# Token-major block 0 of an S5 + GEGLU kernel: tile 3 taken last and from its DMA-turned form, its weight columns loaded in smaller pieces and on a second queue

## The chip, the cores and the metric
One core of a Trainium2 chip (trn2) runs the whole program. The metric is device time in microseconds (us); the figure for the kernel before is the median of three runs.

## The reference
One input x of 2048 tokens by 512 features is normalized (layernorm without gain), and three things are added: x itself, a diagonal complex state-space layer (S5), and a GEGLU feed-forward layer. Inputs and output are bfloat16.

```python
def _A_ref(x, ...):                       # S5, P = D = 512
    Lam_bar = jnp.exp(dt * Lam)
    B_bar = ((Lam_bar - 1.0) / Lam)[:, None] * Bmat
    Bu = jnp.einsum("bld,pd->blp", x + 0j, B_bar)
    h = Lam_bar[None, :] * h + Bu[:, t, :]          # for each t of 2048
    ...
    return 2.0 * jnp.einsum("blp,dp->bld", hseq, Cmat).real + x * Dskip

def _B_ref(x, w_gate, w_up, w_down):      # 512 -> 1376 -> 512
    return (_gelu(x @ w_gate) * (x @ w_up)) @ w_down

xn = _layernorm(x, axis=-1)
return x + _A_ref(xn, ...) + _B_ref(xn, ...)
```

## The kernel before
The 2048 tokens are four blocks of 512, each of four tiles of 128 tokens. For each block TensorE makes the gate and up products (`GU`), the input of the state-space layer (`BU`), and the down product with the state output (`DN`); VectorE runs the recurrence as scans (`CHAIN`), ScalarE applies gelu and empties PSUM.

In blocks 1 to 3, and for the hidden columns from 896 up in block 0, a matmul has the weights as its stationary operand and takes the *turned* normalized block `XNT[b]` (features on partitions). It is made by DMA: VectorE writes the normalized tile `XN` (`norms`, L634), and SyncE issues one DMA transpose per tile (`TR`, L736). That needs the statistics (`stats`, L615 and L616), the root on GpSimd (`root`, L621 to L623) and the reciprocal (`recip`, L627) first.

Block 0 is the start of the program, where the DMA engines bring the weights. Its hidden columns 0 to 895 are therefore made *token-major*: the tile of tokens is the stationary operand, and the weights stream past it, gate and up side by side in one PSUM bank. Four column groups `FR` of 256, 256, 256 and 128 are numbered u = 0 to 3. The tile is not yet normalized for this: VectorE only subtracts the mean (`cent` L962 for tiles 0 and 1, `sub` L951 for 2 and 3), TensorE turns it in four 128x128 pieces (`cent_T`, L684), ScalarE copies the turned tile to `XC` (L689), and the reciprocal of the standard deviation `rss[j]` goes in as the scale of gelu (L721) and of the multiply behind it (`GT_evac`, L724). `GT_k` (L701) is one matmul with one of the four slices of 128 features, so that it can start as soon as that slice of the weights has come; columns 0 to 511 of tiles 0 to 2 are made so. `GT_mm` (L712) is one accumulation of four matmuls. Ten of them follow: tile 3, columns 0 to 511, then columns 512 to 767 and 768 to 895 of tiles 0, 1, 2, 3. The hidden result goes to `H0` and is turned by DMA later (`H0_T`).

The gate and up weights come in parts: columns 0 to 511 slice by slice (`ld_wk`, L488, 128 KB each), then the ranges of `FC` (`ld_w`, L493): columns 512 to 895 (384 KB each) and 896 to 1375 (480 KB each, in `load_W`). All of these are issued by SyncE, and so run on DMA queue q1; the X tiles 1 and 2 and three parameter rows are issued by ScalarE, on q10. Behind the weights SyncE issues the transpose of the parameters (L515), the four DMA transposes of block 0's tiles, x of block 1 (L482) and the transposes of B (L526).

Order: the program lists operations, and a scheduler at build time gives each engine a fixed order. TensorE and SyncE keep the order of the listing; VectorE, ScalarE and GpSimd are ordered by modelled due times, save where `order_behind` (and `ch`, which chains VectorE's early operations) ties one behind another. Waits are semaphores; an engine that waits holds all that is behind it in its own order.

Of the kernel before, what the change touches and what calls it, by code (L numbers as in the profile page):

```python
# [9 lines left out]
ALU = mybir.AluOpType  # L10
ACTF = mybir.ActivationFunctionType
# [335 lines left out]
L, D, P, F = 2048, 512, 512, 1376  # L347
NT, NB, KD, KP, KF = 16, 4, 4, 4, 11
# [6 lines left out]
def d_pe(n_list):  # L355
    return sum(n / 2.4 + 2.5 for n in n_list)
def d_dve_tt2x(n): return 100.0 + 0.52 * n
def d_dve_1x(n): return 100.0 + 1.04 * n
# [3 lines left out]
def d_act(n, ptr=0): return 190.0 + 0.833 * n + 90.0 * ptr  # L362
# [3 lines left out]
def build(nc, ins, out):  # L366
    with ExitStack() as es:
        E = es.enter_context
        S = Sched(nc, es)
# [3 lines left out]
        PS = [E(nc.psum_tensor("PS%d" % i, [128, 512], F32)) for i in range(8)]  # L373
        BANK = [Buf("bank%d" % i, "ps", i, i + 1) for i in range(8)]
# [4 lines left out]
        WG = A.alloc("WG", [KD, F], BF16)  # L379
# [1 line left out]
        assert WG.lo == 0 and WU.lo == WG.hi  # L381
        WGU = arena_t[:, 0:2 * KD * F].rearrange("p (w k f) -> p w k f", w=2, k=KD)
        WD = A.alloc("WD", [KF, D], BF16)
        FC = [(0, 512), (512, 896), (896, F)]
        WGc = [Buf("WGc%d" % i, "sbx", 10 * i, 10 * i + 1) for i in range(KD + 2)]
        WUc = [Buf("WUc%d" % i, "sbx", 100 + 10 * i, 101 + 10 * i) for i in range(KD + 2)]
        wdeps = lambda Wc, ft: Wc[0:KD] if ft < 4 else [Wc[KD + (ft > 6)]]
        WDc = [Buf("WDc%d" % i, "sbx", 200 + 10 * i, 201 + 10 * i) for i in range(2)]
        XNT_all = A.alloc("XNT", [NB, KD, TB_], BF16)
        XNT = ring(XNT_all, "XNT", NB)  # L390
# [97 lines left out]
            return S.dma(lambda e: e.dma_start(W.ap[:, k, f0:f1], src[128 * k:128 * (k + 1), f0:f1]),  # L488
                         256 * (f1 - f0), writes=[Wc[k]], tag="ld_w")

        def ld_w(W, Wc, src, n):
            f0, f1 = FC[n]
            return S.dma(lambda e: e.dma_start(W.ap[:, :, f0:f1], src[:, f0:f1].rearrange("(k p) f -> p k f", p=128)),  # L493
                         1024 * (f1 - f0), writes=[Wc[KD + n - 1]], tag="ld_w")

        def ld_x0(j, queue="sync", after=()):
            return S.dma(lambda e, j=j: e.dma_start(X[j].ap, x2[128 * j:128 * (j + 1), :]), 128 * 1024, writes=[X[j]], tag="ld_x0", queue=queue, after=after)  # L497
# [2 lines left out]
        for k in range(KD):  # L500
# [1 line left out]
                ld_x0(k)  # L502
            ld_wk(WG, WGc, ins["B_w_gate"], k)
            ld_wk(WU, WUc, ins["B_w_up"], k)
        ld_w(WG, WGc, ins["B_w_gate"], 1)
        ld_w(WU, WUc, ins["B_w_up"], 1)

        def load_par():
            for q, nm in enumerate(("A_log_dt", "A_Lambda_re", "A_Lambda_im")):
# [17 lines left out]
                      1.4 * 512 * 1024, writes=[b_], tag="tr_" + nm, issue=3000.0)  # L527

        def load_W():
            ld_w(WG, WGc, ins["B_w_gate"], 2)  # L530
            ld_w(WU, WUc, ins["B_w_up"], 2)

        def load_B():
            load_T([A.sub(BBT_all, "BBTc%d" % c, c) for c in range(2)], ("A_B_re", "A_B_im"))
# [78 lines left out]
        def stats(b, j):  # L613
            tt = 4 * b + j
            return (S.order_behind(V(lambda e: e.bn_stats(ST[tt].ap, X[tt].ap), d_dve_1x(512), [X[tt]], [ST[tt]], "bnst"), GATE["hm"] if b else None),  # L615
                    V(lambda e: e.bn_aggr(MVt[b][j].ap, ST[tt].ap), D_TINY, [ST[tt]], [MVt[b][j]], "bnag"))  # L616
# [9 lines left out]
        def recip(qb, rq):  # L626
            return V(lambda e: e.reciprocal(rq.ap, qb.ap), 150, [qb], [rq], "rq")  # L627

        def norms(b, js, mn, rq, j0):
            last = None  # L630
            for j in js:
                tt, i = 4 * b + j, j - j0
                xs = XN[tt % 8]
                last = S.order_behind(V(lambda e, tt=tt, i=i, xs=xs: e.tensor_scalar(  # L634
                    xs.ap, X[tt].ap, mn.ap[:, i:i + 1], rq.ap[:, i:i + 1], ALU.subtract, ALU.mult),
                  d_dve_ts4x(512), [X[tt], mn, rq], [xs], "ln_n"), last)
            return last
# [66 lines left out]
        def GT_mm(j, u, bank):  # L704
            f0, f1 = FR[u]
            w = f1 - f0
            dst = PS[bank][:, 0:2 * w].rearrange("p (w f) -> p w f", w=2)

            def f(e):
                ins_ = None  # L710
                for k in range(KD):
                    ins_ = e.matmul(dst, XCd(j, k), WGU[:, :, k, f0:f1], start=(k == 0), stop=(k == KD - 1))  # L712
                return ins_
            PE(f, d_pe([2 * w] * KD), wdeps(WGc, 2 * u) + wdeps(WUc, 2 * u) + XCs[j], [BANK[bank]], "GT")

        def GT_evac(j, u, bank):
            f0, f1 = FR[u]
            w = f1 - f0
            GATE["nh"] = kk = (GATE["nh"] + 1) % 3
            sc, rb = rss[j]  # L720
            GATE["last_gelu"] = S.order_behind(ACT(lambda e: e.activation(GG[kk].ap[:, 0:w], PS[bank][:, 0:w], ACTF.Gelu_apprx_tanh, scale=sc),  # L721
                                                   d_act(w, 1), [BANK[bank], rb], [GG[kk]], "gelu"), GATE.get("last_gelu"))
            hp = Buf("H0_%d_%d" % (j, u), "sb", H0[j].lo + 2 * f0, H0[j].lo + 2 * f1)
            GATE["hm"] = S.order_behind(V(lambda e: e.scalar_tensor_tensor(H0[j].ap[:, f0:f1], PS[bank][:, w:2 * w], sc, GG[kk].ap[:, 0:w], ALU.mult, ALU.mult),  # L724
                                          d_dve_1x(w), [BANK[bank], GG[kk], rb], [hp], "hmul"), GATE.get("hm"))

        def H0_T():
            for j in range(4):
# [4 lines left out]
        def TR(b, js=range(4)):  # L733
            for j in js:
                tt = 4 * b + j
                S.dma(lambda e, b=b, j=j, tt=tt: e.dma_start_transpose(  # L736
                    XNT[b].ap[:, :, 128 * j:128 * (j + 1)], XN[tt % 8].ap),
                    1.6 * 128 * 1024, reads=[XN[tt % 8]], writes=[XTk[b][j]], tag="tr_x%d" % b, issue=1280.0)
# [67 lines left out]
        def GU_rest(b):  # L806
            k2, ft = b % 2, KF - 1
            f0, m = 128 * ft, FROWS[ft]
            for i in range(2):
                bank = next_bank()  # L810

                def f(e, i=i, bank=bank):
                    ins_ = None
                    for j in (2 * i, 2 * i + 1):
                        dst = PS[bank][:, 256 * (j % 2):256 * (j % 2) + 2 * m].rearrange("p (w f) -> p w f", w=2)
                        for dk in range(KD):
                            ins_ = e.matmul(dst, XNT[b].ap[:, dk, 128 * j:128 * (j + 1)], WGU[:, :, dk, f0:f0 + m],  # L817
                                            start=(dk == 0), stop=(dk == KD - 1))
                    return ins_
                PE(f, d_pe([2 * m] * 8), [WGc[KD + 1], WUc[KD + 1]] + XTr(b), [BANK[bank]], "GR%d" % b)  # L820
                GATE["nh"] = kk = (GATE["nh"] + 1) % 3
                g_, u_ = (PS[bank][:, :].rearrange("p (j x) -> p j x", j=2)[:, :, w * m:(w + 1) * m] for w in range(2))
                gs, us = (t[kk].ap[:, 0:2 * m].rearrange("p (j f) -> p j f", j=2) for t in (GG, UPB))
                GATE["last_gelu"] = ACT(lambda e, g_=g_, gs=gs: e.activation(gs, g_, ACTF.Gelu_apprx_tanh),
                                        d_act(2 * m), [BANK[bank]], [GG[kk]], "gelu", after=GATE["before_gelu"])
                ACT(lambda e, u_=u_, us=us: e.activation(us, u_, ACTF.Copy), d_act(2 * m), [BANK[bank]], [UPB[kk]], "evU")
                V(lambda e, i=i, gs=gs, us=us: e.tensor_tensor(HR.ap[:, 2 * i:2 * i + 2, 0:m], gs, us, ALU.mult),
                  d_dve_tt2x(2 * m), [GG[kk], UPB[kk]], [HRp[i]], "hmul")
            S.dma(lambda e: e.dma_start_transpose(HTt[k2][ft].ap.rearrange("p (j t) -> p j t", j=4), HR.ap),
                  1.2 * 128 * 1024, reads=HRp, writes=[HTt[k2][ft]], tag="tr_h%d" % b, issue=1200.0)  # L830
# [116 lines left out]
        def ch(*ops):  # L947
            for op in ops:
                tail_op[0] = S.order_behind(op, tail_op[0])
        def sub(j):  # L950
            return V(lambda e: e.tensor_scalar(XN[j].ap, X[j].ap, MVt[0][j].ap[:, 0:1], None, ALU.subtract),  # L951
                     d_dve_ts4x(512), [X[j], MVt[0][j]], [XN[j]], "sub")
# [39 lines left out]
        ch(*stats(0, 1))  # L992
        op, mn0, qb0, rq0 = root(0, 0, 3)
        ch(op)
        ch(*stats(0, 3)); ch(sub(3))
        ch(recip(qb0, rq0))
        op, mn3, qb3, rq3 = root(0, 3, 4)
        ch(op)
        rss = [(rq0.ap[:, i:i + 1], rq0) for i in range(3)] + [(rq3.ap, rq3)]
        for j in range(2):  # L1000
            ch(norms(0, [j], mn0, rq0, 0))
        ch(recip(qb3, rq3))
        TR(0, [0, 1])
        ks(1, 2, [0, 1])
        ks(2, 2, [0, 1])
        for j in range(3):
            GT_k(3, j, 0, [0, 1])
            if j == 0:
                cent_T(3, 0, 4, 6)
            GT_k(3, j, 1, [0, 1])  # L1010
            for u in range(2):
                GT_evac(j, u, acc(j, u))
        for (j, u), bank in zip([(3, 0), (3, 1), (0, 2), (0, 3), (1, 2), (1, 3), (2, 2), (2, 3), (3, 2), (3, 3)],
                                (6, 7, 0, 1, 2, 3, 4, 5, 0, 7)):
            GT_mm(j, u, bank)
            GT_evac(j, u, bank)
        rstate["n"] = 2
        norms(0, [2], mn0, rq0, 0)
        norms(0, [3], mn3, rq3, 3)
        TR(0, [2, 3])  # L1020
        ld_x(1)
        params()
        tables_dve(None)
# [87 lines left out]
```

## Time and profile before
| | us |
|---|---|
| median of three runs | 176.86 (176.77 to 177.54) |
| profiled execution, time | 177.26 |
| profiled execution, span | 175.9 |
| DMA traffic of block 0's stage, 4.4 to 13.2 | 281 and 322 GB/s in the two slices |
| last gate load (480 KB, issued 6.50), to landing | 6.8 |
| last up load (480 KB, issued 7.04), to landing | 7.6 |

Times inside the profile count from the start of the span. In the DMA view "to landing" counts from the start of the issue on the engine to the last of the data's arrival. SPq and ACTq are the sequencers of SyncE and ScalarE that issue DMAs; q1 and q10 are their DMA queues. Lines are those of the kernel before unless the text says otherwise; the change moves `GT_mm`'s matmul to L713 and `GU`'s to L851.

### The profile page before, as it was taken

How to read it: one execution, taken by the hardware profiler on the slowest of the kernel's cores; microseconds unless marked ns; L12 is line 12 of the kernel's file. 1: busy time of each engine (PE TensorE's matmuls, PEld its weight loads, DVE VectorE, ACT ScalarE, POOL GpSimd, SP SyncE). 2: the span in 40 equal slices, each digit the busy share in tenths (PEclk: the TensorE clock that was granted, in tenths of full speed). 3: DMA queues.
4: the chain of work that ended last, by engine and by line, in shares of the span. 5: the costliest groups of instructions: out<-in, count | busy, mean ns of one | idle time of the engine just before them, and what ended most of it. 6: DMA issues, size and time to landing. Idle time of an engine off the chain costs nothing.

```text
span 175.9 us, 2549 instructions
## 1 busy us (share of the span) xinstructions
PE 172.8 (98%) x903; PEld 85.4 (49%) x903; DVE 159.7 (91%) x279; ACT 95.8 (54%) x187; POOL 10.7 (6%) x24
## 2 busy tenths in 40 slices
PE   7999999999999999999999999999999999999995
PEld 2645664744544444444644444444464444444454
DVE  6797999987999989889899999989999899999941
ACT  5367668999766899383676793000667970000000
POOL 3132120211000000002200000000000000000000
DMA  5999989975899000002015000002004000000311
GB/s 144 281 322 154 216 136 203 174 132 114 162 270 270 11 0 2 0 30 75 18 33 112 5 0 4 0 0 89 30 0 34 0 0 0 0 0 4 119 62 60
DMA packets 32421, 14.36 MB, mean 82 GB/s; under 512 B 23737, under 2 KB 32409, under 8 KB 32409
## 3 DMA queue, kind: packets, MB, share of 16 engines
q1 hardware_dynamic: 31952, 13.84, 36.9%
q10 hardware_dynamic: 456, 0.36, 0.6%
q8 instruction: 7, 0.11, 0.3%
q14 instruction: 6, 0.04, 0.1%
HBM read 6.46 MB, written 2.10 MB: 49 GB/s over the span
## 4 chain that ended last, share of the span: by engine, by line
PE 95%; DMA 2%; SPq 1%; issue 0%; DVE 0%
PE PS L885 37%; PE PS L843 32%; PE PS L749 16%; PE PS L712 4%; PE PS L817 3%; PE PS L701 2%; DMA arena<-in_B_w_up_dram 2%; SPq L488 1%; PE PS L684 0%; SPq L497 0%; DVE arena L903 0%
## 5 line engine op out<-in xcount | busy, mean ns | idle before, releaser
L885 PE MATMUL PS<-arena 128*128 128x512 bf16 (+3 forms) x323 | 66.2, 366 | 0.0
L843 PE MATMUL PS<-arena 128*128 128x512 bf16 (+1 forms) x272 | 58.1, 373 | 0.0
L885 PEld LDWEIGHTS PS<-arena 128*128 128x128 bf16 (+1 forms) x323 | 30.8, 98 | 35.2
L843 PEld LDWEIGHTS PS<-arena 128*128 128x128 bf16 x272 | 26.5, 98 | 29.5
L787 DVE TENSOR_TENSOR_SCAN arena<-arena 128x512 bf16<-128x512 f32 x32 | 38.9, 1256 | 0.0
L859 ACT ACTIVATE arena<-PS 128x512 bf16<-128x512 f32 x33 | 19.8, 599 | 26.2 <-DVE arena L903 16.7
L749 PE MATMUL PS<-arena 128*128 128x512 bf16 (+1 forms) x144 | 28.3, 355 | 0.1
L863 ACT ACTIVATE arena<-PS 128x512 bf16<-128x512 f32 x33 | 19.8, 599 | 5.4 <-PE PS L843 5.4
L749 PEld LDWEIGHTS PS<-arena 128*128 128x128 bf16 x144 | 14.0, 98 | 13.7 <-DMA arena<-arena 0.6
L877 ACT ACTIVATE PS<-arena 128x512 f32<-128x512 bf16 (+2 forms) x17 | 9.6, 582 | 19.7 <-DVE arena L903 19.0
L758 ACT ACTIVATE arena<-PS 128x512 bf16<-128x512 f32 x32 | 17.6, 597 | 1.6 <-PE PS L749 1.6
L903 DVE TENSOR_TENSOR arena<-PS,arena 128x512 bf16<-128x512 f32 (+2 forms) x17 | 10.9, 654 | 6.4 <-PE PS L885 6.4
L865 DVE TENSOR_TENSOR arena<-arena 128x512 bf16<-128x512 bf16 x33 | 13.2, 419 | 2.1 <-ACT arena L863 2.0
L776 DVE TENSOR_TENSOR arena<-arena 128x4096 bf16<-128x4096 bf16 (+1 forms) x5 | 9.2, 1859 | 0.4 <-ACT arena L611 0.4
L799 DVE TENSOR_TENSOR arena<-arena 128x4096 bf16<-128x4096 bf16 x4 | 9.2, 2291 | 0.1
L774 DVE TENSOR_TENSOR arena<-arena 128x4096 bf16<-128x4096 bf16 (+1 forms) x5 | 9.2, 1861 | 0.0
L800 DVE TENSOR_TENSOR arena<-arena 128x4096 bf16<-128x4096 bf16 x4 | 9.1, 2287 | 0.0
L615 DVE BATCH_NORM_STATS2 arena<-arena 128x6 f32<-128x512 bf16 x12 | 7.8, 685 | 0.9 <-DMA arena<-in_A_x_dram 0.7
L721 ACT ACTIVATE arena<-PS,arena 128x256 bf16<-128x256 f32 (+1 forms) x16 | 6.5, 450 | 3.3 <-DVE arena L621 1.5
L712 PE MATMUL PS<-arena 128*128 128x512 bf16 (+1 forms) x40 | 7.1, 336 | 0.0
L701 PE MATMUL PS<-arena 128*128 128x256 bf16 (+1 forms) x36 | 6.2, 308 | 0.2 <-DMA arena<-in_B_w_up_dram 0.2
L724 DVE SCALAR_TENSOR_TENSOR arena<-PS,arena 128x256 bf16<-128x256 f32 (+1 forms) x16 | 6.2, 444 | 0.0
(95 smaller groups left out, 124.2 us busy)
## 6 DMA issues: line engine op xcount, KB each, us to landing
out_dram<-arena SPq DMA_DIRECT2D x15, 128.0 KB, 1.7
arena<-in_A_x_dram SPq DMA_DIRECT2D x3, 512.0 KB, 6.3
arena<-in_B_w_down_dram SPq DMA_DIRECT2D x1, 1280.0 KB, 8.8
arena<-in_B_w_gate_dram SPq DMA_DIRECT2D x4, 128.0 KB, 3.4
arena<-in_B_w_up_dram SPq DMA_DIRECT2D x4, 128.0 KB, 3.6
arena<-in_B_w_gate_dram SPq DMA_DIRECT2D x1, 480.0 KB, 6.8
arena<-in_B_w_up_dram SPq DMA_DIRECT2D x1, 480.0 KB, 7.6
arena<-arena SPq DMA_TRANSPOSE x25, 3.3
```

The source lines that it names most:

```text
L701: PE(lambda e: e.matmul(dst, XCd(j, k), WGU[:, ws[0]:ws[-1] + 1, k, f0:f1], start=first, stop=k == KD - 1, skip_group_check=True), d_pe([w ...
L712: ins_ = e.matmul(dst, XCd(j, k), WGU[:, :, k, f0:f1], start=(k == 0), stop=(k == KD - 1))
L749: ins_ = e.matmul(PS[bank][:, 128 * j0:128 * j1], BBT[c][dk].ap[:, 128 * s:128 * (s + 1)], XNT[b].ap[:, dk, 128 * j0:128 * j1], start=(dk ...
L758: GATE["evBu"] = ACT(lambda e, bank=bank, k3=k3, s=s, c=c: e.activation(SSc[k3][s][c].ap, PS[bank][:, :], ACTF.Copy), d_act(512), [BANK[ba ...
L787: V(lambda e, g=g, rb=rb, init=init: e.tensor_tensor_scan(g.ap, rb, g.ap, init, ALU.mult, ALU.add), d_dve_scan(512), [g, PA[RRr]] + ([CARc ...
L843: ins_ = e.matmul(PS[bank][0:m, c0:c1], W.ap[:, dk, 128 * ft:128 * ft + m], XNT[b].ap[:, dk, c0:c1], start=(dk == 0), stop=(dk == KD - 1))
L859: GATE["last_gelu"] = ACT(lambda e, bg=bg, kk=kk, m=m: e.activation(GG[kk].ap[0:m, :], PS[bg][0:m, :], ACTF.Gelu_apprx_tanh), d_act(512), ...
L863: ACT(lambda e, bu=bu, kk=kk, m=m: e.activation(UPB[kk].ap[0:m, :], PS[bu][0:m, :], ACTF.Copy), d_act(512), [BANK[bu]], [UPB[kk]], "evU")
L865: V(lambda e, kk=kk, m=m, ft=ft, k2=k2: e.tensor_tensor(HTt[k2][ft].ap[0:m, :], GG[kk].ap[0:m, :], UPB[kk].ap[0:m, :], ALU.mult), d_dve_tt ...
L877: ACT(lambda e: e.activation(PS[bank][:, c0:c1], X[tt].ap[:, c0:c1], ACTF.Copy), d_act(c1 - c0), [X[tt]], [BANK[bank]], "seed")
L885: ins_ = e.matmul(PS[bank][:, c0:c1], l_[:, 128 * j:128 * (j + 1)], r_[:, c0:c1], start=False, stop=last and n == len(ops) - 1, skip_group ...
L903: V(lambda e: e.tensor_tensor(OUTB[ko].ap[:, c0:c1], PS[bank][:, c0:c1], XD[tt].ap[:, c0:c1], ALU.add), d_dve_1x(c1 - c0), [BANK[bank], XD ...
```

## The change
Six edits, all in block 0. (1) The columns 512 to 895 are loaded as 512 to 767 and 768 to 895, two loads for each of gate and up. (2) The up load of columns 896 to 1375 goes from SyncE's queue to ScalarE's, behind the eviction of turned tile 2. (3) Tile 3 is no longer centred by VectorE, turned by TensorE and copied by ScalarE. (4) `GT_mm` of tile 3 takes the DMA-turned, normalized tile, so that its gelu and multiply have no scale. (5) The order of the ten `GT_mm` is: columns 512 to 767 of tiles 0, 1, 2, then 768 to 895 of tiles 0, 1, 2, then tile 3 with all four groups; the banks follow, and the bank counter behind them starts at 0. (6) The tiles' DMA transposes are issued in the order 0, 3, 1, 2. In the fixed order of VectorE, tile 2 is normalized ahead of tile 3, and all four ahead of the first multiply.

```diff
--- before.py
+++ after.py
@@ -381,10 +381,10 @@
         assert WG.lo == 0 and WU.lo == WG.hi
         WGU = arena_t[:, 0:2 * KD * F].rearrange("p (w k f) -> p w k f", w=2, k=KD)
         WD = A.alloc("WD", [KF, D], BF16)
-        FC = [(0, 512), (512, 896), (896, F)]
-        WGc = [Buf("WGc%d" % i, "sbx", 10 * i, 10 * i + 1) for i in range(KD + 2)]
-        WUc = [Buf("WUc%d" % i, "sbx", 100 + 10 * i, 101 + 10 * i) for i in range(KD + 2)]
-        wdeps = lambda Wc, ft: Wc[0:KD] if ft < 4 else [Wc[KD + (ft > 6)]]
+        FC = [(0, 512), (512, 768), (768, 896), (896, F)]
+        WGc = [Buf("WGc%d" % i, "sbx", 10 * i, 10 * i + 1) for i in range(KD + 3)]
+        WUc = [Buf("WUc%d" % i, "sbx", 100 + 10 * i, 101 + 10 * i) for i in range(KD + 3)]
+        wdeps = lambda Wc, ft: Wc[0:KD] if ft < 4 else [Wc[KD + (ft > 5) + (ft > 6)]]
         WDc = [Buf("WDc%d" % i, "sbx", 200 + 10 * i, 201 + 10 * i) for i in range(2)]
         XNT_all = A.alloc("XNT", [NB, KD, TB_], BF16)
         XNT = ring(XNT_all, "XNT", NB)
@@ -488,10 +488,10 @@
             return S.dma(lambda e: e.dma_start(W.ap[:, k, f0:f1], src[128 * k:128 * (k + 1), f0:f1]),
                          256 * (f1 - f0), writes=[Wc[k]], tag="ld_w")
 
-        def ld_w(W, Wc, src, n):
+        def ld_w(W, Wc, src, n, queue="sync"):
             f0, f1 = FC[n]
             return S.dma(lambda e: e.dma_start(W.ap[:, :, f0:f1], src[:, f0:f1].rearrange("(k p) f -> p k f", p=128)),
-                         1024 * (f1 - f0), writes=[Wc[KD + n - 1]], tag="ld_w")
+                         1024 * (f1 - f0), writes=[Wc[KD + n - 1]], tag="ld_w", queue=queue)
 
         def ld_x0(j, queue="sync", after=()):
             return S.dma(lambda e, j=j: e.dma_start(X[j].ap, x2[128 * j:128 * (j + 1), :]), 128 * 1024, writes=[X[j]], tag="ld_x0", queue=queue, after=after)
@@ -502,8 +502,9 @@
                 ld_x0(k)
             ld_wk(WG, WGc, ins["B_w_gate"], k)
             ld_wk(WU, WUc, ins["B_w_up"], k)
-        ld_w(WG, WGc, ins["B_w_gate"], 1)
-        ld_w(WU, WUc, ins["B_w_up"], 1)
+        for n in (1, 2):
+            ld_w(WG, WGc, ins["B_w_gate"], n)
+            ld_w(WU, WUc, ins["B_w_up"], n)
 
         def load_par():
             for q, nm in enumerate(("A_log_dt", "A_Lambda_re", "A_Lambda_im")):
@@ -527,8 +528,7 @@
                       1.4 * 512 * 1024, writes=[b_], tag="tr_" + nm, issue=3000.0)
 
         def load_W():
-            ld_w(WG, WGc, ins["B_w_gate"], 2)
-            ld_w(WU, WUc, ins["B_w_up"], 2)
+            ld_w(WG, WGc, ins["B_w_gate"], 3)
 
         def load_B():
             load_T([A.sub(BBT_all, "BBTc%d" % c, c) for c in range(2)], ("A_B_re", "A_B_im"))
@@ -709,20 +709,28 @@
             def f(e):
                 ins_ = None
                 for k in range(KD):
-                    ins_ = e.matmul(dst, XCd(j, k), WGU[:, :, k, f0:f1], start=(k == 0), stop=(k == KD - 1))
+                    xs = XCd(j, k) if j < 3 else XNT[0].ap[:, k, 128 * j:128 * (j + 1)]
+                    ins_ = e.matmul(dst, xs, WGU[:, :, k, f0:f1], start=(k == 0), stop=(k == KD - 1))
                 return ins_
-            PE(f, d_pe([2 * w] * KD), wdeps(WGc, 2 * u) + wdeps(WUc, 2 * u) + XCs[j], [BANK[bank]], "GT")
+            PE(f, d_pe([2 * w] * KD), wdeps(WGc, 2 * u) + wdeps(WUc, 2 * u) + (XCs[j] if j < 3 else [XT0[j]]), [BANK[bank]], "GT")
 
         def GT_evac(j, u, bank):
             f0, f1 = FR[u]
             w = f1 - f0
             GATE["nh"] = kk = (GATE["nh"] + 1) % 3
-            sc, rb = rss[j]
-            GATE["last_gelu"] = S.order_behind(ACT(lambda e: e.activation(GG[kk].ap[:, 0:w], PS[bank][:, 0:w], ACTF.Gelu_apprx_tanh, scale=sc),
-                                                   d_act(w, 1), [BANK[bank], rb], [GG[kk]], "gelu"), GATE.get("last_gelu"))
             hp = Buf("H0_%d_%d" % (j, u), "sb", H0[j].lo + 2 * f0, H0[j].lo + 2 * f1)
-            GATE["hm"] = S.order_behind(V(lambda e: e.scalar_tensor_tensor(H0[j].ap[:, f0:f1], PS[bank][:, w:2 * w], sc, GG[kk].ap[:, 0:w], ALU.mult, ALU.mult),
-                                          d_dve_1x(w), [BANK[bank], GG[kk], rb], [hp], "hmul"), GATE.get("hm"))
+            gate, up, g, h = PS[bank][:, 0:w], PS[bank][:, w:2 * w], GG[kk].ap[:, 0:w], H0[j].ap[:, f0:f1]
+            if j < 3:
+                sc, rb = rss[j]
+                fg = lambda e: e.activation(g, gate, ACTF.Gelu_apprx_tanh, scale=sc)
+                fh = lambda e: e.scalar_tensor_tensor(h, up, sc, g, ALU.mult, ALU.mult)
+                rb = [rb]
+            else:
+                fg = lambda e: e.activation(g, gate, ACTF.Gelu_apprx_tanh)
+                fh = lambda e: e.tensor_tensor(h, up, g, ALU.mult)
+                rb = []
+            GATE["last_gelu"] = S.order_behind(ACT(fg, d_act(w, 1), [BANK[bank]] + rb, [GG[kk]], "gelu"), GATE.get("last_gelu"))
+            GATE["hm"] = S.order_behind(V(fh, d_dve_1x(w), [BANK[bank], GG[kk]] + rb, [hp], "hmul"), GATE.get("hm"))
 
         def H0_T():
             for j in range(4):
@@ -817,7 +825,7 @@
                             ins_ = e.matmul(dst, XNT[b].ap[:, dk, 128 * j:128 * (j + 1)], WGU[:, :, dk, f0:f0 + m],
                                             start=(dk == 0), stop=(dk == KD - 1))
                     return ins_
-                PE(f, d_pe([2 * m] * 8), [WGc[KD + 1], WUc[KD + 1]] + XTr(b), [BANK[bank]], "GR%d" % b)
+                PE(f, d_pe([2 * m] * 8), [WGc[KD + 2], WUc[KD + 2]] + XTr(b), [BANK[bank]], "GR%d" % b)
                 GATE["nh"] = kk = (GATE["nh"] + 1) % 3
                 g_, u_ = (PS[bank][:, :].rearrange("p (j x) -> p j x", j=2)[:, :, w * m:(w + 1) * m] for w in range(2))
                 gs, us = (t[kk].ap[:, 0:2 * m].rearrange("p (j f) -> p j f", j=2) for t in (GG, UPB))
@@ -992,32 +1000,31 @@
         ch(*stats(0, 1))
         op, mn0, qb0, rq0 = root(0, 0, 3)
         ch(op)
-        ch(*stats(0, 3)); ch(sub(3))
-        ch(recip(qb0, rq0))
+        S.order_behind(ld_w(WU, WUc, ins["B_w_up"], 3, "scalar"), GATE["evTA"])
+        ch(*stats(0, 3))
         op, mn3, qb3, rq3 = root(0, 3, 4)
         ch(op)
-        rss = [(rq0.ap[:, i:i + 1], rq0) for i in range(3)] + [(rq3.ap, rq3)]
-        for j in range(2):
-            ch(norms(0, [j], mn0, rq0, 0))
+        ch(recip(qb0, rq0))
+        rss = [(rq0.ap[:, i:i + 1], rq0) for i in range(3)]
+        ch(norms(0, [0], mn0, rq0, 0))
+        ch(norms(0, [1], mn0, rq0, 0))
         ch(recip(qb3, rq3))
-        TR(0, [0, 1])
+        ch(norms(0, [3], mn3, rq3, 3))
+        TR(0, [0, 3, 1])
         ks(1, 2, [0, 1])
         ks(2, 2, [0, 1])
         for j in range(3):
             GT_k(3, j, 0, [0, 1])
-            if j == 0:
-                cent_T(3, 0, 4, 6)
             GT_k(3, j, 1, [0, 1])
             for u in range(2):
                 GT_evac(j, u, acc(j, u))
-        for (j, u), bank in zip([(3, 0), (3, 1), (0, 2), (0, 3), (1, 2), (1, 3), (2, 2), (2, 3), (3, 2), (3, 3)],
-                                (6, 7, 0, 1, 2, 3, 4, 5, 0, 7)):
+        for (j, u), bank in zip([(0, 2), (1, 2), (2, 2), (0, 3), (1, 3), (2, 3), (3, 0), (3, 1), (3, 2), (3, 3)],
+                                (6, 7, 0, 1, 2, 3, 4, 5, 6, 7)):
             GT_mm(j, u, bank)
             GT_evac(j, u, bank)
-        rstate["n"] = 2
+        rstate["n"] = 0
         norms(0, [2], mn0, rq0, 0)
-        norms(0, [3], mn3, rq3, 3)
-        TR(0, [2, 3])
+        TR(0, [2])
         ld_x(1)
         params()
         tables_dve(None)
```

## The prediction
> **What bounds the kernel now.** I read the page's busy shares first, then the chain of work that ended last in order of time, then SyncE's timeline and the DMA view in narrow windows. On the page:
>
> ```profile
> PE 172.8 (98%) x903; PEld 85.4 (49%) x903; DVE 159.7 (91%) x279; ACT 95.8 (54%) x187; POOL 10.7 (6%) x24
> ```
>
> TensorE is busy for 172.8 of 175.9 us, so an edit pays only by taking work or a wait from TensorE, and a new TensorE wait is paid almost in full. The chain over the changed stage and its first pause afterwards (start us, length us, what):
>
> ```profile
> 7.86 1.89 PE PS L701 x9
> 9.75 0.34 PE PS L684 x4
> 10.09 1.08 PE PS L701 x5
> 11.16 6.93 PE PS L712 x40
> 18.09 5.20 PE PS L843 x32
> ...
> 31.52 0.12 issue
> ```
>
> L684 x4 is tile 3 being turned on TensorE. L712 x40 are ten whole accumulations (`GT_mm`): 24 matmuls of 512 columns and 16 of 256. Block 0's token-major work ends at 18.09, and what follows runs back to back but for 0.12 us at 31.52. The question is therefore when L843 can start in the changed kernel.
>
> SyncE's timeline (start, length, what) and the DMA view of single issues (size, us from issue to landing) give the data's side:
>
> ```profile
> 4.98 0.45 SPq L488 DMA_DIRECT2D arena<-in_B_w_up_dram  x1
> 5.47 0.43 SPq L493 DMA_DIRECT2D arena<-in_B_w_gate_dram  x1
> 5.95 0.51 SPq L493 DMA_DIRECT2D arena<-in_B_w_up_dram  x1
> 7.82 1.99 SPq L515 DMA_TRANSPOSE arena<-arena  x1
> 10.27 5.15 SPq L736 DMA_TRANSPOSE arena<-arena  x4
> ```
>
> ```profile
> arena<-in_B_w_up_dram SPq DMA_DIRECT2D x1, 128.0 KB, 3.8
> arena<-in_B_w_up_dram SPq DMA_DIRECT2D x1, 384.0 KB, 6.0
> arena<-arena SPq DMA_TRANSPOSE x1, 5.0
> arena<-arena SPq DMA_TRANSPOSE x1, 4.1
> ```
>
> Issue plus landing time: the last 128 KB up chunk arrives at 8.8, the 384 KB up chunk at 11.95. The first two turned tiles, issued at 10.27 and about 11.6, arrive at 15.3 and 15.7: they wait behind 960 KB of weights on the same queue, so their arrival is set by the DMA engines, not by their issue.
>
> **The change, part by part.** *Removed from TensorE:* four turns of tile 3, 0.34 us of the chain. The twelve L701 matmuls around them then follow each other, and the first `GT_mm` could start at 9.75 + 1.08 = 10.83. Forty matmuls remain after it, 6.93 us. With no wait L843 starts at 17.76, a gain of 0.33.
>
> *First new wait, the weights of columns 512 to 767.* Before, the first two `GT_mm` (tile 3, columns 0 to 511) needed only weights long there, and columns 512 and up were first touched at 11.16 + 8 matmuls of 0.217 = 12.9, 0.95 after their arrival at 11.95. Now tile 0 columns 512 to 767 comes first, at 10.83. Its two loads are 256 KB instead of 384 KB, with the same 1024 row pieces. The two old loads took 11.95 - 8.8 = 3.15 us; the new take 2.1 by bytes and 3.15 by pieces. I take 2.4, nearer to bytes, as the share of busy DMA engines follows the bytes moved elsewhere in this stretch. That alone gives 11.2.
>
> Then comes the third up chunk, 480 KB, on ScalarE's queue. It stands behind the last eviction of tile 2 (second L689 of the pair at 7.73) and waits for nothing, so it is issued near 8.0 and moves data from about 9.0, by the 0.9 us between X tile 0's issue at 0.74 and the first DMA traffic. What a second queue does to SyncE's queue can be seen where X tile 2 came on ScalarE's queue. The DMA view of 4.4 to 5.2 (packets, MB, share of 16 engines), and below it that of 5.4 to 6.2:
>
> ```profile
> q1 hardware_dynamic: 163, 0.15, 55.6%
> q10 hardware_dynamic: 126, 0.11, 46.2%
> ```
>
> ```profile
> q1 hardware_dynamic: 265, 0.24, 98.8%
> q10 hardware_dynamic: 5, 0.00, 1.5%
> ```
>
> Beside q10, q1 moves 0.15 MB where alone it moves 0.24, a factor of 0.62. At 9.0 the new chunk still needs 2.2 us alone, 2.2 / 0.62 = 3.5 beside q10; q10's 0.49 MB at 0.11 per 0.8 us last 3.6, so the whole of it is shared. Arrival: 12.5. The ends: by bytes 1.9 / 0.62 gives 12.1, by pieces 13.3; unshared, 10.9. I take 12.4. TensorE then waits 1.6 us at its first `GT_mm`, and the forty matmuls end at 12.4 + 6.93 = 19.3.
>
> The Trainium skill, "DMA: Bandwidth & Descriptors", Queues, rings and completion order, says that each DMA engine takes turns between queue rows packet by packet. By that rule the 960-byte pieces of ScalarE's load would take more than the equal share seen above from 512-byte pieces, and the arrival would be about 12.8, 0.4 later than my sum; no stretch of this trace has unequal pieces on the two queues, so the trace leaves it open; the sum would be 178.4, inside the forecast's own range.
>
> *Second new wait, the turned tile 3.* Its four accumulations come last and need the DMA-turned tile. Up to there TensorE has 3 x 0.87 + 3 x 0.43 = 3.9 us of `GT_mm`, so it asks for it at 14.7 without the first wait and at 16.3 with it. VectorE normalizes tiles 0, 1, 2 and then 3 before the hmuls: reciprocal at 9.55, three L634 to about 10.8, L627 at 10.85, L634 done near 11.4. So the tile is issued second, at about 11.6, where the old second one stood. It arrived at 15.7; q1 ahead of it and q10 together hold the same bytes, but the old pair of 384 KB loads has become four, two of them 128 KB in rows of 256 bytes. The window 14 to 15, nearly all 256-byte pieces of turns, moved at up to 282 GB/s, so these 256 KB take 0.93. With the 2.4 above that is 3.33 against 3.15 for the old pair: 15.9. The ends: by bytes 15.7, and with the first pair by pieces (3.15) 16.6. I take 15.9. This is under the 16.3, so it adds nothing to the sum, but it would bind at 14.7 if the first wait went away.
>
> *Hidden:* SyncE issues two loads more and one fewer at a pitch of 0.48; the PAR transpose moves to about 8.3 and ends at 10.3, where tile 0's turn stood anyway (10.27). ScalarE issues its load in 0.65 us of an idle stretch of 1.46 (before 9.85), and loses one eviction of 0.59. VectorE loses one subtract (0.35); its hmuls start near 11.4 at 0.39 each, and the first bank they must free (0) is asked for after 2 x 0.87 us of `GT_mm`, 12.6 at the earliest, when it is free. The exp of the parameters waits for the PAR transpose (15.0 before, up to 0.8 later), and L558 on VectorE behind it; queued behind L558 are the hmuls of tiles 1 to 3, and their banks 2 to 7 are asked for by L843 after 20. Without that cover each 0.1 of delay costs 0.1. The gelu without scale and the plain multiply are off the path: 0.
>
> *Sum:* 19.3 - 18.09 = +1.2, less the pause of 0.12 at 31.52, which a later TensorE uses up: +1.1 us. The profiled execution took 177.26 with its span of 175.9, so it would be 178.4; from the median of 176.86, which lies 0.4 lower, it is 178.0.
>
> **Rivals.**
> *Not slower: both transfers land in time.* If the chunk is there by 10.83 and the tile by 14.7, the turns' 0.33 and the 0.12 are won: 176.4. For it: a smaller first chunk, and 480 KB taken off the queue ahead of the turned tile. Against it: the unshared bound is already 10.9, and the tile would have to come a full us before the 15.7 of its predecessor in the same place. It decides at 11.16 for the chunk and 15.1 for the tile: later than either, the wait has eaten the 0.33.
> *The tile alone binds.* If the second queue fills idle DMA time (261 GB/s on the mean from 6.2 to 10.0, against 335 from 4.4 to 5.2 with both queues), the chunk lands by 11.5 and the tile at 15.7 to 16. L843 then starts 3.02 us (the last 12 x 0.217 + 4 x 0.105) after the tile: 18.7 to 19.0, +0.5 to +0.8 with the pause: 177.5.
> *The short rows bind.* The two loads of columns 768 to 895 lie ahead of the tile in q1. The window 14 to 15 moved 172 GB/s on the mean, and only 282 in its busy part. At 172 their 256 KB take 1.52: the tile comes at 16.5 to 17.2, say 16.9, and L843 at 19.9: +1.8, less the pause: 178.5.
> The Trainium skill, "DMA: Bandwidth & Descriptors", Specifications, wants pieces of 512 bytes or more for the full rate, a rule that speaks against this load; the 282 GB/s of the trace beside its 305 with long rows (5.4 to 6.2) speaks against much of a loss, and the rival has a chance of 0.1.
>
> **How the numbers follow.** Forecast 0.57 (two waits, 177.5 to 178.7); tile alone 0.2; in time 0.13; short rows 0.1. A measurement here tells 0.5% (0.9 us) from no change, so slower begins at 177.7. Of the forecast 0.8 lies above, 0.46; of the tile alone a quarter, 0.05; the short rows whole, 0.1: slower 0.61. In time is a gain of 0.3% and counts as the same: with the rest of the others, 0.36. Faster by 0.9 us would take more than the turns and all pauses of the stage: 0.03. The range leaves out the lower part of in time and little of the first wait's far end: 176.6 to 179.0. The forecast's own is 177.5 to 178.7.
>
> **What would show it.** L713 (the old L712) starts near 12.4 after a wait for the up load, and L851 (the old L843) near 19.3. ScalarE's load is issued near 8.0. The turned tile 3 lands near 16. No L684 x4 after 9. From L851 on everything is as before, shifted by 1.1. Wrong is: a first `GT_mm` before 11.2, a PE wait of under 0.3 in 10 to 19, or L851 before 18.

## The result, and the profile after

The changed kernel takes 177.75 us (median of 22 runs, 177.03 to 178.67) against 177.09 of the kernel before in the same runs (176.59 to 177.57): a ratio of 1.0037, 95% interval 1.0024 to 1.0051. It is slower by 0.66 us, less than the 0.5% that the prediction took as the bound of what can be told; 22 runs of each tell it. Ratios and intervals leave out slow runs, those more than 1.5% above the fastest of their kernel; only e4 below has any, three of its twelve.

The page of the profiled execution (178.04 us, span 176.7), and TensorE's timeline (start, length, line, count, idle time before and its releaser):

```profile
PE 172.2 (97%) x884; PEld 86.0 (49%) x899; DVE 159.7 (90%) x278; ACT 95.0 (54%) x186; POOL 9.6 (5%) x24
```

```profile
7.62 0.39 PE L684 MATMUL PS<-arena 128*128 128x128 bf16 x4
7.85 3.13 PE L701 MATMUL PS<-arena 128*128 128x256 bf16 x14
10.81 4.06 PE L713 MATMUL PS<-arena 128*128 128x512 bf16 x24
15.93 3.20 PE L713 MATMUL PS<-arena 128*128 128x512 bf16 x16 [1.05 <-DMA arena<-arena]
18.96 5.36 PE L851 MATMUL PS<-arena 128*128 128x256 bf16 x31
```

TensorE has four matmuls less to do (899, of which 884 left a record) and is idle longer. The turn of tile 3 is gone, and the first `GT_mm` starts at 10.81. Then TensorE stands for 1.05 us ahead of tile 3's sixteen matmuls. The chain of what ended last shows the wait from the DMA's side, and where block 0's token-major work ends (19.13, against 18.09 before; the chain counts a matmul from the end of the one before it, the timeline from its own start, so that the same L851 stands there at 18.96):

```profile
11.73 4.15 DMA arena<-arena
15.88 0.05 issue
15.93 3.20 PE PS L713 x16
19.13 1.75 PE PS L851 x16
```

The next L851 of the chain begins at 39.50, against 38.74 before, a delay of 0.76: of the 1.04, 0.28 is taken up between. The pause of 0.12 that the kernel before had at 31.52 is part of that; the rest was not traced. The ends of the two spans differ by 0.8.

The data's side, by the DMA view of single issues: the two pieces of columns 512 to 767 (issued at 5.48 and 5.96), and the up load on ScalarE's queue (8.05):

```profile
arena<-in_B_w_gate_dram SPq DMA_DIRECT2D x1, 256.0 KB, 3.8
arena<-in_B_w_up_dram SPq DMA_DIRECT2D x1, 256.0 KB, 4.2
...
arena<-in_B_w_up_dram ACTq DMA_DIRECT2D x1, 480.0 KB, 6.6
```

The chunk arrives at 10.2, 0.6 ahead of its first use. The second queue came too late to hurt it: it has no traffic in the DMA view of 8.4 to 10.0 (the first line below), and half of it from 10.5 to 13.0:

```profile
q1 hardware_dynamic: 1208, 0.45, 108.4%
```

```profile
q10 hardware_dynamic: 459, 0.43, 54.1%
q1 hardware_dynamic: 504, 0.42, 49.3%
```

### The profile page after: what moved, and what is told of

It is laid out like the page before. It is cut to its first block, busy times and chain, and to the rows that moved or that the text cites. A ratio compares the mean times of both kernels' runs of the same rounds, so it can differ in the third digit from the quotient of the medians.

```text
span 176.7 us, 2528 instructions
## 1 busy us (share of the span) xinstructions
PE 172.2 (97%) x884; PEld 86.0 (49%) x899; DVE 159.7 (90%) x278; ACT 95.0 (54%) x186; POOL 9.6 (5%) x24
## 4 chain that ended last, share of the span: by engine, by line
PE 87%; DMA 2%; ACT 2%; issue 1%; DVE 0%; DVEq 0%
PE PS L893 37%; PE PS L851 32%; PE PS L757 13%; PE PS L825 3%; DMA arena<-arena 2%; PE PS L713 2%; ACT arena L766 1%; ACT arena L610 1%; DVE arena L726 0%; DVE arena L911 0%; DVEq L341 0%
## 5 line engine op out<-in xcount | busy, mean ns | idle before, releaser
L851 PE MATMUL PS<-arena 128*128 128x512 bf16 (+1 forms) x265 | 57.3, 373 | 0.4
L851 PEld LDWEIGHTS PS<-arena 128*128 128x128 bf16 x272 | 26.6, 98 | 29.5
L757 PE MATMUL PS<-arena 128*128 128x512 bf16 (+1 forms) x142 | 28.1, 355 | 0.1
L757 PEld LDWEIGHTS PS<-arena 128*128 128x128 bf16 x144 | 14.1, 98 | 13.3
L713 PE MATMUL PS<-arena 128*128 128x512 bf16 (+1 forms) x40 | 7.3, 337 | 1.1 <-DMA arena<-arena 1.1
L713 PEld LDWEIGHTS PS<-arena 128*128 128x128 bf16 x40 | 3.8, 98 | 4.5 <-DMA arena<-arena 1.3
L825 PE MATMUL PS<-arena 128*128 128x192 bf16 x64 | 5.9, 246 | 0.0
```

What stands on the lines that cost most here:

```text
L713: ins_ = e.matmul(dst, xs, WGU[:, :, k, f0:f1], start=(k == 0), stop=(k == KD - 1))
L757: ins_ = e.matmul(PS[bank][:, 128 * j0:128 * j1], BBT[c][dk].ap[:, 128 * s:128 * (s + 1)], XNT[b].ap[:, dk, 128 * j0:128 * j1], start=(dk ...
L851: ins_ = e.matmul(PS[bank][0:m, c0:c1], W.ap[:, dk, 128 * ft:128 * ft + m], XNT[b].ap[:, dk, c0:c1], start=(dk == 0), stop=(dk == KD - 1))
```

## The experiments

In all kernels below but the loads-only pair, every engine's order is that of the changed kernel except for the loads that are named; they were moved after the orders had been fixed. Ratios are to the kernel before on the same chip, whose median was 177.17 (e1 to e4), 177.10 (e5 to e8) and 177.04 us (e9 to e12); they were not taken from the two medians, whose quotient is at times another (1.0062 for e5, where the ratio is 1.0080).

**Without the tile wait (e1).**
```diff
-                    xs = XCd(j, k) if j < 3 else XNT[0].ap[:, k, 128 * j:128 * (j + 1)]
+                    xs = XCd(min(j, 2), k)
...
+            if o.tag == "GT":
+                o.deps = [d for d in o.deps if d.tag != "tr_x0"]
```


> The changed kernel, with tile 3's four accumulations reading tile 2's centred, TensorE-turned copy instead of their own DMA-turned tile (so tile 3's hidden columns 0 to 895 are not those of tile 3); every engine's order and every load stay. Theory, the tile wait: the 1.05 us that TensorE waits ahead of tile 3 is the whole loss. Then the wait is gone, the second group of L713 follows the first without a gap, L851 starts near 17.8 to 18.0 instead of 18.96, and the time is 176.7 to 176.9, 0.2 to 0.4 below the kernel before (the turns that were removed). Rival, the loads: the new pieces and the second queue hold TensorE up elsewhere; then at most half of the loss goes, and the time is 177.3 or more.

177.20 us, ratio 1.0002 (0.9986 to 1.0017). TensorE's timeline has all forty matmuls in one piece:

```profile
11.12 7.09 PE L713 MATMUL PS<-arena 128*128 128x512 bf16 x40
18.05 5.36 PE L851 MATMUL PS<-arena 128*128 128x256 bf16 x31
```

The loss is gone with the wait, while every load stays as it was, so the wait is the loss. But the gain did not come: the interval's lower end is a gain of 0.25 us, short of the 0.33 of the turns. Both theories missed, the tile wait by its gain.

**The loads alone (e2 and again e10).**
```diff
-        FC = [(0, 512), (512, 896), (896, F)]
+        FC = [(0, 512), (512, 768), (768, 896), (896, F)]
...
+        S.order_behind(ld_w(WU, WUc, ins["B_w_up"], 3, "scalar"), GATE["evTA"])
```


> The kernel before with only the loads of the change: the second column range in two pieces for gate and up, the last up range on ScalarE's queue behind the eviction of tile 2; tile 3 is turned on TensorE and the order of the accumulations is the old one. Tile wait: nothing waits for it, 177.1 as before (within 0.2), L843 starts at 18.1. Loads: part or all of the loss of 0.7 shows, 177.4 to 177.8.

> The kernel before with only the changed loads, a second time, since its interval (0.9977 to 1.0002) just touches no change. If the loads themselves are worth something (the turned tiles and B's turn come earlier, and the pause of 0.12 near 31.5 goes), the ratio is again 0.9985 to 0.9995, 176.9 to 177.0. If not, 1.000.

176.97 us, 0.9989 (0.9977 to 1.0002); the second time 176.98, 1.0001 (0.9990 to 1.0012). Smaller pieces and a second queue, without tile 3's wait on the DMA, cost nothing that these runs can tell, and gain 0.4 us at the very most.

**The up load early on ScalarE's queue (e6).** It stands behind the first eviction instead of the sixth.
```diff
 ScalarE: L689 (tile 0)
+ScalarE: up load, columns 896 to 1375
 ScalarE: L689 x5
-ScalarE: up load, columns 896 to 1375
```

> The changed kernel, with ScalarE's up load issued behind its first eviction (near 4.1) instead of its sixth (8.05). It tests the first wait of the prediction: the price of a second queue beside SyncE's weights. Theory, the late start: the wait did not come because the load's first data moved 2.2 us after its issue, when the chunk of columns 512 to 767 had landed. Issued at 4.1 it moves from about 6.3, beside the chunk: the chunk lands 1.0 to 1.5 later than 10.2, at 11.2 to 11.8, TensorE waits 0.4 to 1.0 ahead of L713 or already in L701, and tile 3 still lands near 15.9, so that the two waits together are worth about what the one was: 177.6 to 178.0. Rival, spare DMA time: two queues move more than one, the chunk lands by 10.8 and nothing waits ahead of L713: 177.6.

178.39 us, 1.0078 (1.0057 to 1.0098). ScalarE issues the load at 4.09. The DMA view of 6.4 to 8.0, when both queues had data under way, and TensorE:

```profile
q10 hardware_dynamic: 295, 0.28, 55.6%
q1 hardware_dynamic: 184, 0.17, 37.7%
```

```profile
12.04 7.09 PE L713 MATMUL PS<-arena 128*128 128x512 bf16 x40 [0.26 <-DMA arena<-in_B_w_up_dram]
18.96 5.36 PE L851 MATMUL PS<-arena 128*128 128x256 bf16 x32
```

The load's data ran from about 6.3 to 9.9, beside the slices and the chunk. The chunk landed at 11.9, and L713 starts 1.2 later than in the changed kernel; tile 3, asked for at 16, is there (it landed at 15.4). This is the first wait of the prediction, with the second one hidden behind it. The profiled execution is this kernel's fastest (178.02); its median lies 0.4 above, higher than expected.

**The up load back on SyncE's queue (e7 and again e12).**
```diff
 SyncE: gate load, columns 896 to 1375
+SyncE: up load, columns 896 to 1375
 SyncE: parameters' transpose, turns of tiles 0, 3, 1, 2
-ScalarE: up load (behind L689 x6)
```

> The changed kernel with the up load of columns 896 to 1375 back on SyncE's queue, in its old place behind the gate load; everything else as changed. Bytes alone: the same 960 KB are ahead of the turned tile, it lands at 15.6 to 16.0 and the wait of about 1 us stays: 177.6 to 177.9. If ScalarE's queue was what held the tile, it lands by 15.0 and the time is 177.1 or less. The spread of the single times should be that of the kernel before (about 1 us), not that of the changed one (1.6).

> The run with the up load back on SyncE's queue, another look. Its profile was its fastest execution (177.16, tile 3 landed at 14.9, wait 0.40), its median 177.9. Bytes alone: an execution near the median has the turned tile at 15.6 to 16.0 and a wait of about 1 us ahead of the second group of L713, with no second queue running.

177.92 us, 1.0047 (1.0030 to 1.0063), which overlaps the changed kernel's interval: the second queue was not what the time was lost to. The first profile was the kernel's fastest execution (177.16, a tile wait of 0.40). The second look, a single execution of 177.72, was nearer the median, and shows *both* predicted waits without a second queue:

```profile
11.02 4.06 PE L713 MATMUL PS<-arena 128*128 128x512 bf16 x24 [0.41 <-DMA arena<-in_B_w_up_dram]
15.52 3.20 PE L713 MATMUL PS<-arena 128*128 128x512 bf16 x16 [0.44 <-DMA arena<-arena]
18.56 5.36 PE L851 MATMUL PS<-arena 128*128 128x256 bf16 x32
```

The expectation missed twice: the tile came at 15.5 and the wait was 0.44 and not 1, with as much ahead of L713; and the single times spread nearly as widely as the changed kernel's (177.16 to 178.56), so ScalarE's queue does not account for the spread.

**The gate load behind the first two turns (e3 and again e11).**
```diff
-SyncE: gate load, columns 896 to 1375 (ahead of the parameters' transpose)
 SyncE: parameters' transpose, turns of tiles 0, 3
+SyncE: gate load, columns 896 to 1375
 SyncE: turns of tiles 1, 2
```


> The changed kernel, with the gate load of columns 896 to 1375 (480 KB) issued by SyncE behind the DMA transposes of tiles 0 and 3 instead of ahead of them; all else in its place. Theory, shared engines: all bytes that are under way ahead of the turned tile delay it, whichever queue they are on. 480 KB less at about 340 GB/s is 1.4 us less: tile 3 arrives at 14.5 to 14.9, TensorE waits 0.2 or less, 176.7 to 177.0. Rival, the queue: only what is ahead on its own queue counts; the same here. Rival, the turn itself: its issue and its own latency set the 15.9; then nothing moves, 177.7.

> The run with the gate load behind the first two turns, another look. Its profile had no wait at tile 3 and a span of 175.6, its twelve times had a median of 177.5. An execution near the median should show a wait that the first profile had not, of 0.4 to 1.0 us: at tile 3 if the up load on ScalarE's queue holds the turn, at L851 or L757 if the gate load, tiles 1 and 2 or B come late.

177.53 us, 1.0025 (1.0006 to 1.0044). Tile 3 was in time in both profiles: 480 KB fewer ahead of it do bring it forward (it landed at 13.9 and 14.3), which rules out the turn's own issue and latency as what set 15.9. The time did not follow. The first profile, an execution of 176.99, has no wait at all; the second (177.76) has one where block 0's BU starts:

```profile
11.16 7.09 PE L713 MATMUL PS<-arena 128*128 128x512 bf16 x40
...
25.01 14.22 PE L757 MATMUL PS<-arena 128*128 128x512 bf16 x80 [0.25 <-DMA arena<-in_A_B_re_dram]
```

L757 began at 25.01 where before L749 stood at 24.45: B's turn, at the end of SyncE's queue, came late.

**The up load late on ScalarE's queue (e4), and the same load behind the two turns on SyncE's (e8).**
```diff
-ScalarE: up load, columns 896 to 1375 (behind L689 x6)
+ScalarE: up load (e4, behind the sixth gelu)
+SyncE: up load (e8, between the turns of tiles 0, 3 and of 1, 2)
```

> The changed kernel, with the up load of columns 896 to 1375 (480 KB) issued by ScalarE behind the sixth gelu (about 12.5) instead of behind the eviction of tile 2 (8.05); all else in its place. Shared engines: 480 KB less under way, tile 3 arrives at 14.5 to 14.9 and the wait goes, 176.7 to 177.0, as with the gate load. The queue: the load was on the other queue, so tile 3 still arrives near 15.9 and the wait of about 1 us stays, 177.6 to 177.8.

> The changed kernel with the up load of columns 896 to 1375 on SyncE's queue behind the DMA transposes of tiles 0 and 3 (issued near 12.9); the gate load stays ahead of them. Same bytes ahead of tile 3 and nearly the same time of issue as in the run with the up load late on ScalarE, only the queue differs. Held turn: no second queue is running, tile 3 lands at 13.9 to 14.5, in time for its accumulations near 14.7; L851 starts near 17.8, and the time is 176.6 to 176.9, 0.2 to 0.5 below the kernel before, with little spread. Bytes alone, and the late up load's tile at 16.8 a chance of that execution: the same here, 176.7 to 178.

e4: 178.10 us over the nine runs that count, 1.0035 (1.0002 to 1.0067); its twelve single times go from 176.57 to 181.03, their median is 178.44. e8: 177.65, 1.0034 (1.0021 to 1.0047), 177.21 to 178.21. In e4's profile the turn of tile 3 takes longest of all (chain):

```profile
11.59 4.80 DMA arena<-arena
16.43 3.20 PE PS L713 x16
```

Its DMA view of 13.6 to 14.6, when the up load had begun to move, shows SyncE's queue at a stand and the engines far from full:

```profile
DMA packets 134, 0.13 MB, mean 128 GB/s; under 512 B 1, under 2 KB 134, under 8 KB 134
q10 hardware_dynamic: 133, 0.13, 68.8%
q1 hardware_dynamic: 1, 0.00, 0.1%
```

The turn got through at 16.4, with the load's end (12.35 + 4.2 = 16.55). In e8 the same bytes, issued 0.66 us later (13.01) on SyncE's queue, leave tile 3 in time, and L713 x40 runs from 10.78 in one piece. So in e4's execution the tile stood while the other queue's load ran, and on one queue it did not. That rests on one execution of each, and e4's spread says that not every execution has it. But e8 is no faster. Its chain:

```profile
16.82 8.00 DMA arena<-in_A_B_re_dram
24.82 0.05 issue
24.87 14.18 PE PS L757 x80
```

One load more between the turns puts B's turn at 16.82 instead of the changed kernel's 16.29, it lands at 24.82 instead of 23.62, and TensorE waits for that instead.

**Both late (e5).** The gate load as in e3 and the up load as in e4.

> The changed kernel with both late loads moved: the gate load of columns 896 to 1375 behind the DMA transposes of tiles 0 and 3 on SyncE, the up load behind the sixth gelu on ScalarE. Theory, the held turn: a DMA transpose cannot pass while a plain load runs on the other queue, and it needs all DMA engines to be through with what came before. Tiles 0 and 3 have nothing ahead of them but the first chunks and land at 12.9 to 13.4, before the up load's first data near 14: no wait at tile 3. The other two tiles are held behind both loads and land after 17.5, so that L851 waits up to 0.5: 176.8 to 177.4. Rival, bytes alone: the same tile 3, the other two by 17.0, no wait: 176.7.

178.19 us, 1.0080 (1.0052 to 1.0109). Tile 3 was in time; then L851 stood 1.04. TensorE's timeline, and the turn of tile 1 (issued at 13.12) in the DMA view:

```profile
18.90 5.36 PE L851 MATMUL PS<-arena 128*128 128x256 bf16 x32 [1.04 <-DVE arena L730]
```

```profile
arena<-arena SPq DMA_TRANSPOSE x1, 5.6
```

L851's first products need tiles 0 and 1 and the gate load. The gate load landed at 18.0, tile 1 behind it at 18.7, and L851 starts 0.2 later. The VectorE operation that the profile names as releaser, L730, is the multiply of tile 3, which L851's first bank does not wait for. So the wait came where the held turn expected it, and was twice the 0.5; by bytes alone there would have been none.

**Without the tile wait and without B's (e9).** As e1, and in block 0:
```diff
-BBT[c][dk].ap[:, 128 * s:128 * (s + 1)]
+(WG.ap[:, dk, 128 * s:128 * (s + 1)] if b == 0 and c == 0 else BBT[c][dk].ap[:, 128 * s:128 * (s + 1)])
```

> The run without the tile wait (tile 3's accumulations read tile 2), and in addition the first four state-input units of block 0 (BU, real part of B) read gate weights in place of the DMA-turned B, so that TensorE does not wait for that transpose near 24.5 (their results are left out of the computation). Theory, the next wait: without the tile wait the time came to 177.2 and not to 176.8, since B's turn, pushed back by the turns and loads ahead of it, then ends the stage. Without it the turns' 0.33 show: 176.7 to 176.95, a ratio of 0.9975 to 0.999. Rival, the early weights: TensorE reaches L713 only when the early weights let it, the turns it no longer makes were cover for those, and the time stays at 177.1 to 177.3.

177.16 us, 1.0000 (0.9987 to 1.0013). The theory of B's turn as the one next wait falls: without it the gain still did not show. Its profile (177.81, the slowest of its executions) has 0.17 at L713 for the up chunk and 0.61 at L851:

```profile
18.75 5.36 PE L851 MATMUL PS<-arena 128*128 128x256 bf16 x32 [0.61 <-DVE arena L602]
```

```profile
arena<-arena SPq DMA_TRANSPOSE x1, 5.3
```

The second line is again tile 1's turn, issued at 13.28: it landed at 18.56, and L851 starts 0.19 later, as it does in e5 (18.70 and 18.90) and in e8 (17.80 and 17.99). The releaser that the profile gives, L602, makes tables that L851 does not read; the chain, which goes through it, leads back to the transpose of the parameters (`9.37 6.54 DMA arena<-arena`, L516 of the changed kernel), which is not the cause either. So in this execution the next delivery in line, tile 1, bound.

## Why the prediction was right, and which step of it failed

By its own signs the forecast was wrong in one place: a first `GT_mm` before 11.2 was to tell against it, and the first `GT_mm` started at 10.81. The wait of over 0.3 and L851 after 18 were as it said.

*The turns, 0.33.* They are gone, and L713 started at 10.81, where 10.83 was written. As a gain they were over-sized: e1 and e9, with no tile wait, stand at 1.0002 and 1.0000, and their lower ends leave at most 0.25. L713's start in profiles of the changed order was 10.62 to 11.16 (e6 apart), L712's in the old order 10.98 to 11.36, so the early weights move this point by as much as the turns are worth. Where the rest went was not settled; e9's profile shows 0.61 at tile 1, but that is its slowest execution.

*The first wait, 1.6.* This is the step that failed. Two terms were off. The second queue's first data was put at 9.0, 0.9 after its issue; it came at about 10.1, 2.0 after. And the chunk's two loads took 10.2 - 8.4 = 1.8 instead of 2.4, faster even than by bytes (2.1); what was ahead of them was there at 8.4 and not at 8.8. Either alone would have shortened the wait; together they removed it in the profiled execution. The mechanism itself holds: with the load moved into the chunk's way (e6) L713 starts 1.2 late. The price of sharing was put too low, too: there q1 moved 0.17 MB in 1.6 us, a factor of 0.35 against the 0.24 per 0.8 us alone, where 0.62 was written. And e12 has 0.41 of the wait with all loads on one queue. It is a wait that comes and goes with the early loads, not one that every execution pays.

*The second wait.* The tile was put at 15.9 and landed at 15.88, but that is luck: two errors in the terms cancel. Columns 512 to 895 were all there at 11.3, 0.6 earlier than the 11.95 of the kernel before, where the sum had them 0.2 later. The two loads of 480 KB behind them then took until 14.9, 3.6 us, where the kernel before took 2.7 (11.95 to 14.63), a term that the sum took over as it was. In the other profiles these two loads took 2.8 us behind the loads ahead of them with both on one queue (e7, e12), and 2.7 to 4.5 with one on each (e1, e2, e9, e10); in single executions, then, the second queue sped them up nowhere and often slowed them.

The tile's wait was said to bind if the first wait went away, asked for at 14.7; it was asked for at about 14.9 and bound for 1.05. The rival "the tile alone binds" is what happened, its 177.5 against 177.75 measured, and L843's successor at 19.13 against 18.7 to 19.0, though not for its reason: the chunk was early because the second queue had not begun, not because it filled idle time. That the forecast's 178.0 is near is luck as well: its two waits overlapped, and the second, which it priced at nothing, moved L851 to 19.13 where the first was to move it to 19.3.

*Where the edit was free.* ScalarE issued in 0.40 of its idle stretch, and VectorE's four normalizations were through at 11.4, as written. The short rows of 256 bytes cost little: 1.16 us for both pieces against the 0.93 written, and they were there 0.6 ahead of the old pair of loads all the same. (The 282 GB/s behind the 0.93 was a usual slice of its view, not the top, which is 318.)

*Short rows, and two queues at once.* In the changed kernel the DMA view of 9.6 to 10.1, nearly all 256-byte pieces of these loads, has 261 GB/s, that of 8.0 to 9.0, nearly all 512-byte pieces, 287. The Trainium skill, "DMA: Bandwidth & Descriptors", Specifications, asks for pieces of 512 bytes and more; the rule's sign shows, at 9%, a size that did not matter here. From 10.5 to 13.0, with 960-byte pieces on both queues for the most part, q10 and q1 moved 0.43 and 0.42 MB. The turn-taking of the queues (the Trainium skill, "DMA: Bandwidth & Descriptors", Queues, rings and completion order), by which the prediction let 960-byte pieces take more than 512-byte ones, was not put to the test: the two hardly met in the changed kernel.

## What to carry to other kernels

A step moved from a full engine onto a DMA pays only if the result arrives before its consumer, and behind a backlog of loads its arrival is the backlog's end, not its issue: add up all bytes ahead, on every queue, and compare with the time at which the consumer asks. A second queue did not shorten that sum here, and moving one load behind the critical one hands its wait to whoever needs that load, or what is behind it, next: of four such moves here (e3, e4, e8, e5) none came out clearly below the changed kernel, and e5 came out above it. Where many deliveries are within a few tenths of their use, one profile shows one execution's wait only; look at several before naming the bound, and hold the releaser that a profile names against what the waiting instruction reads.

## What the runs showed of the hardware that was not expected

A load on ScalarE's idle queue moved its first packet between 1.1 and 2.4 us after its issue, over the ten profiles that have it there, while SyncE's queue was busy; an estimate from the first load of the program (0.9) was too short. A DMA transpose beside a plain load on the other queue came to a stand in one execution: one packet of it in 1.0 us, at 128 GB/s in all (e4). And while the turns were queued behind the last of the loads the engines ran nearly empty: in the changed kernel 97 GB/s from 13.5 to 14.5,

```profile
DMA packets 269, 0.10 MB, mean 97 GB/s; under 512 B 220, under 2 KB 269, under 8 KB 269
```

a good microsecond ahead of the tile's arrival. What held them there was not tried apart.
